# Four edits to the last tenth of an attention and spectral-mix kernel: spectra in tiles of their own, made in spare banks, a first step by halves, each step stored by itself

## The chip, the cores and the metric

One core of a Trainium2 chip. The metric is the device time of one execution in microseconds, the median of several; lower is better. Verdicts use a threshold of 2%. Executions of one kernel spread by 0.6 to 3.4 us, so effects of a few tenths are read from the traces.

## The reference, cut to what matters

Sparse attention over q, k, v (8 batches, 8 heads, 576 positions) gives x of shape (8, 576, 512). Then a spectral layer and a channel mix:

```python
X = np.fft.rfft(x, axis=1)
# 64 modes: Y[:, m] = X[:, m] @ (w_r[m] + i w_i[m])
y = np.fft.irfft(Y, n=S, axis=1)
u = x + y
return (u + np.maximum(u @ w_ch, 0.0)).astype(np.float32)
```

The weights w_r and w_i are 2 x 64 matrices of 512 x 512 in fp32, so most of the time goes into loading them. When the last of them are in, a tail remains: the last spectra, their share in each output row, the relu, the add, and 9.44 MB of stores.

## The kernel before: the parts that matter

The tail works in 20 items. An item is a tile t (128 rows, t = 0 to 3) of two batches, or the last 64 rows (t = 4) of two batches in one tile. Tiles t and t+1 hold the even and the odd rows of one stretch of 256, so partition p of a pair has rows 2p and 2p+1, which lie side by side in DRAM. For each item two PSUM tiles are filled, v (before the relu) and u:

```python
def v_early(k, stop=False):          # own rows, kept in SBUF, through an identity matmul
    vps[k] = psum(("v", "v2")[k % 2], pair=True)
    v_own(k, stop)
def u_early(k): ...                  # the same for u
def new_rows(k, acc, spectra): ...   # share of the last 16 modes, 32-row matmuls

def v_done(k): ...                   # ACT: rl = relu(v), PSUM to SBUF
def u_done(k):                       # DVE: osb = u + rl, then the store
    ...
    if t % 2 == 0:
        osbs[P] = pw.tile([128, 2, 2, DM], FP, tag="w", name="osb")
    osb = osbs[P]
    nc.vector.tensor_tensor(out=osb[:, :, t % 2], in0=up, in1=rls.pop(k), op=AluOp.add)
    for j in range(2):
        dst = out[2 * P + j, ds(128 * (t - t % 2), 256), :].rearrange("(p i) e -> p i e", i=2)
        if k < 4:
            nc.sync.dma_start(dst[:, t % 2], osb[:, j, t % 2])    # rows of 2 KB
        elif t % 2:
            nc.sync.dma_start(dst, osb[:, j])                     # rows of 4 KB, once t and t+1 are in
```

The last spectra, z (times w_ch) and y, for two groups of four batches:

```python
def spec_last(bq, kind):
    both = psum(kind, pair=True)
    spec_mm(3, bq, both[:, 1], both[:, 0])         # z, then y
    act_copy(zzs[bq], both[:, 0])
    nc.vector.tensor_copy(out=yys[bq], in_=both[:, 1])

spec_last(0, "v2")
new_rows(0, vps[0], zzs); new_rows(0, ups[0], yys); v_done(0); u_done(0)
v_early(1); new_rows(1, vps[1], zzs); v_done(1)
spec_last(1, "u")
for k in range(2, LAST + 2):
    v_early(k); u_early(k - 1)
    new_rows(k, vps[k], zzs); new_rows(k - 1, ups[k - 1], yys)
    v_done(k); u_done(k - 1)                       # bounds of k cut here
```

PSUM holds one "v", one "v2" and two "u" tiles of two banks each. Output tiles share five buffers with the weights.

The softmax here doesn't subtract the row's maximum and nothing guards it: scores larger than these inputs give would overflow.

## Time and profile before

| | before |
|---|---|
| time | 435.77 us median (435.15 to 436.52, 3 runs) |
| span of the profiled run | 433.8 us |
| last weights land | 393.92 us |
| last add on DVE ends | 426.75 us |

How to read it: the page divides the span into 40 slices and gives for each the share of time in which the 16 DMA engines were busy (in tenths) and what they moved.

```profile
DMA  8999999999999999999999999999999999991688
GB/s 171 209 212 212 213 213 212 212 211 213 213 212 215 213 213 216 212 215 212 213 212 215 213 213 214 213 214 213 213 213 214 213 214 214 213 187 28 243 323 306
```

The row is full to slice 36: the DMA loads weights without a pause, falls to 28 GB/s in slice 37 while the last spectra are made, and then moves stores, busy for 60 to 80% of each of the last three slices. Only the last four slices can change.

### The profile page before, as it was taken

What the parts mean: (1) busy time and instruction counts of PE and PEld (TensorE: products, weight loads), DVE (VectorE), ACT (ScalarE), POOL (GpSimd) and SP (SyncE); (2) the same over time, 40 slices, a digit from 0 to 9 for tenths busy, and PEclk for the clock granted to TensorE, in tenths of its full rate; (3) what the DMA queues carried; (4) which work ended last, traced back from release to release, by engine and by line L of the source; (5) the groups of instructions that cost most, each with busy time, mean ns of one, the idle gap of its engine ahead of it and who ended that gap; (6) DMA issues with size and microseconds to landing.
All of it is one profiled execution on the core that took longest, in us unless ns stands there. A gap on an engine that the chain in (4) does not pass through costs nothing. (4 is left out here: it accounts for less than half of the span.)

```text
span 433.8 us, 12282 instructions
## 1 busy us (share of the span) xinstructions
PE 347.5 (80%) x5424; PEld 241.5 (56%) x5424; DVE 239.1 (55%) x463; ACT 204.1 (47%) x355; POOL 106.6 (25%) x188
## 2 busy tenths in 40 slices
PE   1987878779988887987487677888799859997992
PEld 1865767558767675776354455655457525554330
DVE  2788768835425444543114355846576455564793
ACT  1587768644545544556141324422343345443671
POOL 5432332322423222222222222222123213210000
PEclk9999989966969998899655899989889959999996
DMA  8999999999999999999999999999999999991688
GB/s 171 209 212 212 213 213 212 212 211 213 213 212 215 213 213 216 212 215 212 213 212 215 213 213 214 213 214 213 213 213 214 213 214 214 213 187 28 243 323 306
DMA packets 29284, 92.18 MB, mean 212 GB/s; under 512 B 4080, under 2 KB 5104, under 8 KB 29232
## 3 DMA queue, kind: packets, MB, share of 16 engines
q0 software_dynamic: 24704, 81.28, 94.5%
q1 hardware_dynamic: 3872, 9.72, 6.0%
q8 instruction: 42, 0.69, 0.6%
q10 hardware_dynamic: 656, 0.41, 0.5%
q14 instruction: 10, 0.08, 0.0%
HBM read 163.22 MB, written 9.44 MB: 398 GB/s over the span
## 5 line engine op out<-in xcount | busy, mean ns | idle before, releaser
L552 PE MATMUL y<-X,wt 128*128 128x16 f16 (+1 forms) x2048 | 82.9, 192 | 30.1 <-DMA wt<-in_moe_w_i_dram 27.5
L552 PEld LDWEIGHTS <-wt 128*128 128x128 f16 (+1 forms) x2048 | 73.3, 101 | 42.4 <-issue 31.8
L201 POOL DMA_DIRECT2D wt<-in_moe_w_r_dram x62 | 36.6, 590 | 173.9 <-PE y L552 93.7
L650 PE MATMUL sc<-w_cp,xT 128*128 128x512 f16 (+1 forms) x160 | 46.7, 419 | 0.0
L201 POOL DMA_DIRECT2D wt<-in_moe_w_i_dram x60 | 35.6, 594 | 43.8 <-DMA wt<-in_moe_w_i_dram 33.4
L659 ACT ACTIVATE v<-sc 128x512 f16<-128x512 f32 x32 | 19.1, 597 | 54.2 <-PE sc L650 54.1
L476 ACT ACTIVATE PL<-sc 128x480 f16<-128x480 f32 (+1 forms) x48 | 27.3, 579 | 33.6 <-PE sc L462 33.4
L660 DVE COPY xo<-tp 128x512 f16<-128x512 f16 x32 | 22.1, 691 | 30.2 <-PE tp L658 30.0
L255 DVE TENSOR_TENSOR xb<-av,rec 90x256 f16<-90x256 f32 (+2 forms) x80 | 36.0, 450 | 2.7
L254 DVE RECIPROCAL rec<-av 90x4 f32<-90x4 f32 (+2 forms) x80 | 14.6, 183 | 33.8 <-PE av L491 22.2
L407 DVE COPY qT<-tp 128x576 f16<-128x576 f16 x16 | 12.0, 758 | 36.6 <-PE tp L400 33.6
L265 ACT ACTIVATE v<-tp 128x640 f16<-128x640 f16 (+1 forms) x24 | 19.4, 808 | 19.7 <-PE tp L434 16.5
L882 DVE TENSOR_TENSOR xo<-u,xo 128x1024 f16<-128x1024 f32 x16 | 19.6, 1225 | 15.2 <-PE u L690 15.1
L400 PE MATMUL tp<-cI_s,ring 64*64 64x64 f16 x864 | 25.0, 204 | 2.0 <-issue 1.2
L365 ACT ACTIVATE PL<-sc 90x360 f16<-90x360 f32 (+1 forms) x48 | 22.8, 490 | 6.6 <-PE sc L358 5.6
L265 ACT ACTIVATE v<-v 128x1024 f16<-128x1024 f32 x16 | 16.4, 1024 | 17.8 <-PE v L690 17.8
L446 PE MATMUL sc<-cMl_s,cI_s 128*128 128x480 f16 (+1 forms) x48 | 21.2, 441 | 3.3 <-ACT X L265 1.6
L400 PEld LDWEIGHTS <-ring 64*64 64x64 f16 x864 | 19.5, 117 | 6.9 <-issue 3.2
L290 PE MATMUL tp<-cI_s,ring 72*128 72x72 f16 x256 | 15.1, 206 | 10.2 <-DMA ring<-in_v_dram 8.6
L519 PEld LDWEIGHTS <-xb 108*128 108x128 f16 (+2 forms) x176 | 15.3, 106 | 12.8 <-DVE xb L255 8.2
L940 ACT ACTIVATE rl<-v 128x1024 f32<-128x1024 f32 (+1 forms) x20 | 18.8, 939 | 7.2 <-PE u L928 5.4
L462 PEld LDWEIGHTS <-kz 128*128 128x128 f16 x160 | 15.3, 111 | 11.6 <-issue 8.1
(114 smaller groups left out, 703.7 us busy)
## 6 DMA issues: line engine op xcount, KB each, us to landing
wt<-in_moe_w_r_dram POOLq DMA_DIRECT2D x62, 512.0 KB, 17.5
wt<-in_moe_w_i_dram POOLq DMA_DIRECT2D x60, 512.0 KB, 19.0
out_dram<-osb SPq DMA_DIRECT2D x12, 512.0 KB, 3.8
ring<-in_v_dram POOLq DMA_DIRECT2D x8, 288.0 KB, 13.3
ring<-in_q_dram POOLq DMA_DIRECT2D x8, 288.0 KB, 13.6
ring<-in_k_dram POOLq DMA_DIRECT2D x8, 288.0 KB, 13.3
out_dram<-osb SPq DMA_DIRECT2D x8, 256.0 KB, 2.6
ring<-in_v_dram POOLq DMA_DIRECT2D x3, 512.0 KB, 14.9
```

Source lines behind the costliest of these rows:

```text
L201: nc.gpsimd.dma_start(dst, rows)
L255: nc.vector.tensor_tensor(out=dst, in0=val.rearrange("p h (q c) -> p h c q", c=4), in1=rec[0:n, 0:pieces] .to_broadcast((n, pieces, 64)) . ...
L265: nc.scalar.activation(out=out, in_=in_, func=ACTF.Copy)
L365: nc.scalar.activation(out=PS[0:n, ds(POFF[t], 4 * n)], in_=scp[0:n, 0 : 4 * n], func=ACTF.Exp, scale=SCALE,)
L400: nc.tensor.transpose(tp[ds(64 * hp, 64), ds(64 * i, 64)], qn[ds(64 * hp, 64), ds(64 * (9 * g + i), 64)], idn[ds(64 * hp, 64), ds(64 * hp, ...
L446: nc.tensor.matmul(scp[:, 0 : n * times].rearrange("p (h x) -> p h x", h=times), idn, mask_rows("cMl", n, times), start=True, stop=False,)
L476: nc.scalar.activation(out=dst, in_=src, func=ACTF.Exp, scale=SCALE)
L552: nc.tensor.matmul(yv[:, mi, e, :], wt[pr, XC[c], ds(128 * e, 128)], Xh[half][pr, c, :, :, m], start=(c == 0), stop=(c == 3),)
L650: nc.tensor.matmul(vp[pr, :], xT[:, ch, cols], w_chs["cp"][:, ch, :], start=(ch == 0), stop=(ch == 3),)
L659: nc.scalar.activation(out=v0[pr], in_=vp[pr, :], func=ACTF.Copy)
L660: nc.vector.tensor_copy(out=xo[pr].rearrange("p (h q c) -> p h q c", h=2, c=4), in_=tp[pr, 0:512].rearrange("p (h c q) -> p h q c", h=2, c=4),
L882: nc.vector.tensor_tensor(out=xo, in0=up[:, 0:n], in1=xo, op=AluOp.add)
```

## The change

Its intent: start the second half of item 0 sooner, give the copies of z and y a tile each so that they don't wait for each other, use banks that stand half empty for the second spectra, and send every item out as soon as it is added. The core of the diff:

```diff
     for bq in range(2):
-        for t in (0, 1, 4, 2, 3) if bq == 0 else (0, 1, 2, 3, 4):
-            items += [(2 * bq, t), (2 * bq + 1, t)]
+        own_t = ((0, 1, 4, 2, 3), (0, 1, 4, 2, 3)) if bq == 0 else ((0, 1, 4, 2, 3), (0, 1, 2, 3, 4))
+        for ts in zip(*own_t):
+            items += [(2 * bq + j, t) for j, t in enumerate(ts)]
 ...  v_done
+        for j in [slice(0, 1), slice(1, 2)] if k == 0 else [slice(0, n)]:
+            nc.scalar.activation(out=rls[k][:, j], in_=vp[:, j], func=ACTF.Relu)
 ...  u_done
+        osb = pw.tile([128, n, DM], FP, tag="w", name="osb")
+        for j in [slice(0, 1), slice(1, 2)] if k == 0 else [slice(0, n)]:
+            nc.vector.tensor_tensor(out=osb[:, j], in0=up[:, j], in1=rl[:, j], op=AluOp.add)
+            if t < 4:
+                rows = out[:, ds(128 * (t - t % 2), 256), :].rearrange("b (p i) e -> p b i e", i=2)
+                bs = slice(2 * P + j.start, 2 * P + j.stop)
+                nc.sync.dma_start(rows[:, bs, t % 2], osb[:, j])
 ...  the tail (spec_z and spec_y are the two halves of spec_mm)
-    spec_last(0, "v2")
+    zp, yp = psum("v2", pair=True)[:, 0], psum("u", pair=True)[:, 0]
+    spec_z(3, 0, zp)
+    spec_y(3, 0, yp)
+    act_copy(zzs[0], zp)
+    nc.vector.tensor_copy(out=yys[0], in_=yp)
     new_rows(0, vps[0], zzs)
+    v_done(0)
+    v_early(1)
     new_rows(0, ups[0], yys)
-    v_done(0)
     u_done(0)
-    v_early(1)
     new_rows(1, vps[1], zzs)
     v_done(1)
-    spec_last(1, "u")
+    u_early(1)
+    new_rows(1, ups[1], yys)
+    u_done(1)
     for k in range(2, LAST + 2):
         if k <= LAST:
             v_early(k)
+        if k == 4:
+            held = vps[k][:, 1]
+            spec_z(3, 1, held)
+        if k == 5:
+            held = vps[k][:, 1]
+            spec_y(3, 1, held)
 ...
+        if k in (4, 5):
+            act_copy((zzs, yys)[k - 4][1], held)
```

## The prediction

> **What bounds the kernel now.** I read the page first, then the chain of waits over the last 54 us, the timeline of each engine there, and the busy time by stretches. The page shows the DMA engines full from the second slice to slice 36 of 40, on the weight loads of the `wt` tiles. The change touches nothing before the last weights, so only what follows can move. Where that begins and what follows is in the chain (start us, us, what):
>
> ```profile
> 382.10 11.81 DMA wt<-in_moe_w_i_dram
> 393.92 0.14 issue
> 394.05 0.64 PE y L552 x16
> ...
> 396.89 0.86 PE v L675 x4
> 397.76 0.24 PE v L671 x4
> 398.00 0.03 ACTq L265
> 398.02 0.04 issue
> 398.07 0.61 ACT zz L265
> 398.67 0.02 issue
> 398.70 0.70 DVE yy L992
> 399.40 0.04 issue
> 399.44 0.39 PE u L928 x2
> ...
> 426.06 0.69 DVE osb L947
> ```
>
> The last weights land at 393.92, the span ends at 433.8: the change lives in 40 us, 9% of the kernel. Two things are to be seen. From 397.76 to 399.44 PE makes the last spectra (L675 z, L671 y), ACT copies z, DVE copies y, strictly one after the other, although the copies read different banks. And the chain stops at the last add, which ends at 426.75, 7 us before the span does. Those 7 us are stores. The stretches show it (us from the start; PE, PEld, DVE, ACT, POOL busy; clock; DMA share; GB/s):
>
> ```profile
> 402.50:403.50 1.00, 1.00 (x9) 0.36 (x8) 0.95 (x2) 0.41 (x2) 0.00 (x0) 1.00 0.99 381
> 406.70:409.80 3.10, 3.10 (x17) 0.92 (x16) 1.88 (x4) 1.90 (x3) 0.00 (x0) 1.00 1.01 382
> 414.50:429.00 14.50, 10.95 (x68) 3.29 (x64) 11.34 (x11) 8.37 (x9) 0.00 (x0) 0.92 1.01 404
> 410.20:412.00 1.80, 1.80 (x14) 0.51 (x12) 1.73 (x2) 1.38 (x2) 0.00 (x0) 1.00 0.89 256
> 412.10:414.20 2.10, 2.10 (x12) 0.63 (x12) 1.94 (x3) 1.81 (x2) 0.00 (x0) 1.00 0.00 0
> 429.60:432.00 2.40, 0.00 (x0) 0.00 (x0) 0.00 (x0) 0.00 (x0) 0.00 (x0) 0.50 0.94 271
> ```
>
> The stores are 9.44 MB. They begin at 402.3, stand wholly still at 412.1 to 414.2 (the kernel there holds a row-pair tile back until both halves are added), and from 414.5 to 429.0 the DMA is full at 404 GB/s, while PE ends at 425.8. So the end is set by when the first store starts, how long the DMA idles between stores, and how fast it moves the bytes. Three speeds are to be seen: 381 to 382 GB/s for rows of 2 KB (the first stores), 404 for rows of 4 KB (the pair stores), 256 to 271 for the 64-row last tiles (t = 4). The costs of the work that feeds them:
>
> ```profile
> L958 DVE TENSOR_TENSOR osb<-u,rl 128x1024 f32<-128x1024 f32 x16 | 19.6, 1224 | 2.6 <-ACT rl L940 0.8 <-PE u L928 0.6
> L940 ACT ACTIVATE rl<-v 128x1024 f32<-128x1024 f32 x16 | 16.4, 1024 | 5.8 <-PE u L928 4.2 <-PE v L928 1.6
> L947 DVE TENSOR_TENSOR osb<-u,rl 128x512 f32<-128x512 f32 x4 | 2.7, 686 | 0.8 <-issue 0.8
> L940 ACT ACTIVATE rl<-v 128x512 f32<-128x512 f32 x4 | 2.4, 598 | 1.4 <-PE u L928 1.2
> ```
>
> **What the Trainium skill says.** "PSUM — Partial Sum Buffer", Specifications: ScalarE and VectorE may read PSUM in parallel at full bandwidth as long as they do not meet in a bank. The trace of before shows them apart only (zz 398.07 to 398.67, yy from 398.70); the program makes DVE wait for ACT because both copies read one tile. Giving z and y separate tiles should let the copies overlap. "VectorE: DVE Perf Modes", the TRN2 errata section, gives an fp32 tensor_tensor add as (N+151)/0.96 ns: 691 and 1224 at N = 512 and 1024; the rows above say 686 and 1224, so it agrees, and halving one add costs about 0.15 us. "ScalarE: Activation LUTs", What ACT_TABLE_LOAD costs, gives an ACTIVATE with immediates as 186 + 0.833 N ns: 612 and 1039 against 598 and 1024 here; halving costs about 0.17 us. "DMA: Bandwidth & Descriptors", Why small descriptors are slow, gives about 3 cycles a packet beside one per 32 bytes; as an estimate that makes 2 KB rows (64+3)/64 over (128+3)/128 = 2% dearer than 4 KB rows. The trace says 404/382 = 6%. The measurement decides.
>
> **The change part by part.** I took the order of the program and its waits for both kernels and walked them with the trace's durations: matmul pairs of L908 and L917 0.43 us, a pair of L928 0.32, an add 0.11 us after its rows of u end, a store's first bytes 0.8 us after its issue (401.45 to about 402.3).
>
> (1) Tiles of their own. ACT can start on z at 397.83 instead of 398.07 (the y matmuls take 0.24), DVE copies y at 398.07 to 398.76 instead of 398.70 to 399.39. The own rows of item 1 (L908, 0.43) fill PE's wait for yy. Rows of v begin at 398.47 instead of 398.71, rows of u at 399.22 instead of 399.44.
>
> (2) First step by halves. ACT relu 398.90 to 399.50 and to 400.10. DVE adds 399.68 to 400.37 and to 401.06; before, one add ran 400.20 to 401.43. The first 256 KB go out at 400.4 instead of 401.45, the second at 401.1. First bytes: 401.2 instead of 402.3, worth 1.1 us.
>
> (3) Second step at once, last spectra later. Before, PE made the second spectra (1.26 us) and DVE their yy copy (0.69) ahead of item 1's add, which ended at 404.4. After: own rows of u 399.86, relu 400.12 to 401.14, add 401.19 to 402.42: 2.0 us earlier. The second spectra (0.87 + 0.24) move into the half-used banks of items 4 and 5, which have one bank each. The work on PE is the same, so this gain is paid back: walking on, the adds end at 404.22, 406.39, 407.18, 408.48, 410.54 for items 2 to 6, where before they ended at 405.7, 407.0, 407.7, 409.0, 410.9. From item 6 on PE runs at 1.30 us an item in both, 0.3 us ahead of before. DVE loses one 0.69 copy to ACT, which has room (8.37 busy of 14.5). The last add ends at about 426.3 instead of 426.75.
>
> (4) Each step stored by itself. Item 6 is stored at 410.56 instead of 413.49, so the 2.1 us of standstill go. Against that all whole items now have 2 KB rows: 512 KB at 385 GB/s are 1.36 us, at 407 they were 1.29.
>
> The DMA's ledger. Before: first byte 402.3, idle 1.3 + 0.45 + 2.1 = 3.9 to 4.0, busy 8 x 0.68 + 12 x 1.29 + about 4.2 for the last tiles = 25.1, with small gaps 25.7; last byte 432.0. After: first byte 401.2; idle 0.65 (402.6 to 403.25), 0.45 (404.6 to 405.05), 0.8 (406.4 to 407.2), 0.9 (410.5 to 411.4) = 2.8; busy 16 x 1.36 + 4.2 = 26.0; last byte 430.0. The gain is 1.1 (start) + 1.2 (idle) - 0.9 + 0.6 (rows of 2 KB, less the small gaps that the before ledger carries and the after ledger does not) = 2.0 us. From item 6 on the ledger has the DMA without a pause for 18 to 19 us: it makes 1.36 an item where PE and DVE need 1.30, so 0.3 us more or less on the engines changes nothing at the end. What follows the last byte (432.0 to 433.8) stays. 435.77 - 2.0 gives 433.7.
>
> **The rivals.** First: the end follows the engines, and their 0.4 us is all there is (435.3). For it: DVE is busy 11.34 of the 12.25 us in which it still worked in that stretch, and PE all but without a pause. Against it: 7 us of stores after the last add. Second: the 2 KB rows eat the gain. All 8.4 MB at 382 would be 22.0 us against 20.9 now; if the three-level stores also issue slowly (the 64-row ones took SP 0.54 us and more, the 128-row ones 0.33), or with the DMA below 380, the end comes at 435 to 436. Nothing of before has this form of store, so I can't exclude it. Third: output tiles. Before used 12 of them, after uses 20 from the same five buffers, so an add must wait for the store five items back. By my ledger store k-5 lands 0.8 to 1.5 us before add k needs its buffer, so no wait; if it comes, the DMA has four stores queued at that time and the end hardly moves, by 0.5 us at most. Fourth, upward: the DMA does better than 385 once stores stand end to end, or idles less early; then 405 GB/s leaves 1.0 us more (432.7).
>
> **Range and chances.** The executions of before spread by 1.4 us, as much as most of what is in question. I take 433.7, with 432.5 (fourth rival and a quicker start) to 435.2 (first or second). A gain of 2% is 8.7 us, more than the 7 us of stores after the last add and over four times my sum: 1 in 100. A loss of 2% would need the stores at about two thirds of their speed: 1 in 100.
>
> **What would show it.** Right: zz and yy copies overlap near 398; the first store at about 400.4; item 1 added by 402.4; no DMA standstill after 411.5; last byte near 430.0 at about 385 GB/s from 411.5 on; the last add near 426.3. Wrong: a wait of the adds for stores; a rate under 375 in that stretch; standing DMA between 404 and 411 of more than 3 us; PE held at the own rows of u in items 2 to 5 by more than 0.3 us; or weights that land at another time than 393.9, which the change gives no reason for.

## The result, and the profile after

433.81 us median (432.90 to 434.26, 4 runs) against 436.14 us for before on the same chip (435.15 to 436.73, 4 runs): 0.9946, interval 0.9920 to 0.9973. By its interval it is a gain of about 0.5%. Ratios are the mean time of one kernel's fast runs over that of the other's of the same rounds, so not quite the ratio of the medians.

The chain of waits of the changed kernel, where the tail begins (start us, us, what):

```profile
393.69 0.64 PE y L552 x16
...
396.45 1.52 PE v L912 x4
397.97 0.88 PE v L669 x4
...
398.92 0.61 ACT zz L265
```

Beside the same lines of before (L675 and L908 there; shown in the prediction), z (L669) starts 1.1 us later although the weights were 0.4 us earlier. The four own-row matmuls of L912 took 1.52 us where before had 0.86: TensorE was at half clock just here. The busy times of the changed kernel show it (us from the start; PE, PEld, DVE, ACT, POOL busy with counts; granted clock; DMA share; GB/s):

```profile
390.80:394.20 3.40, 1.76 (x22) 0.93 (x22) 1.85 (x3) 0.65 (x2) 0.00 (x0) 1.00 0.33 65
394.20:397.70 3.50, 3.50 (x29) 1.59 (x26) 0.29 (x1) 0.00 (x0) 0.00 (x0) 0.51 0.00 0
```

and before in the same places:

```profile
390.80:394.20 3.40, 2.29 (x29) 1.21 (x28) 2.38 (x3) 1.62 (x2) 0.00 (x0) 1.00 0.37 75
394.20:397.70 3.50, 3.50 (x46) 2.07 (x44) 0.29 (x1) 0.00 (x0) 0.00 (x0) 1.00 0.01 1
```

No edit touches that stretch, and a second trace of the changed kernel (below) has the full clock there and is 0.8 us shorter. Half clock comes and goes between traces: those of u_tiles and no_u_own (below) have 3.4 us of it at this place, those of u_spectra and u_halves 6.8 us of it that end at 393.3 and 394.3, and the others none from 385 on until the last matmuls are done. So tails are compared from a mark that this can't reach: the start of the z copy (ACT zz). The copies of the changed kernel overlap now, DVE's start lying 0.18 us after ACT's, and each takes as long as it did alone (0.60 and 0.69 us); ACT's relus and DVE's adds of the end follow:

```profile
398.92 0.60 ACT L265 ACTIVATE zz<-v 128x512 f16<-128x512 f32 x1 [6.57 <-PE v L669]
```
```profile
399.10 0.69 DVE L991 CAST yy<-u 128x512 f16<-128x512 f32 x1 [2.32 <-PE u L676]
400.92 2.42 DVE L954 TENSOR_TENSOR osb<-u,rl 128x512 f32<-128x512 f32 x3 [1.13 <-PE v L932]
...
410.04 10.38 DVE L954 TENSOR_TENSOR osb<-u,rl 128x1024 f32<-128x1024 f32 x8 [0.64 <-PE u L932]
...
421.93 5.79 DVE L954 TENSOR_TENSOR osb<-u,rl 128x1024 f32<-128x1024 f32 x5 [0.64 <-PE u L932]
```

The stores of the changed kernel in the same columns as before:

```profile
411.70:412.20 0.50, 0.50 (x7) 0.10 (x4) 0.50 (x1) 0.50 (x1) 0.00 (x0) 1.00 0.22 57
412.20:423.00 10.80, 10.80 (x66) 3.29 (x64) 9.47 (x9) 7.82 (x9) 0.00 (x0) 1.00 1.00 378
429.50:431.00 1.50, 0.00 (x0) 0.00 (x0) 0.00 (x0) 0.00 (x0) 0.00 (x0) 0.50 0.81 240
```

The 2.1 us of standstill have become a quarter of a microsecond at 412. From then on the DMA is full, at 378 GB/s where before had 404, and the last byte lands at 430.9, 3.2 us after the last add (427.72). DVE's waits hold no store at all (us in total, times, longest):

```profile
...
DVE osb L954 <- PE u L932: 3.2, 5, 1.0
DVE yy L991 <- PE u L676: 2.3, 1, 2.3
DVE osb L954 <- PE v L932: 1.1, 1, 1.1
DVE osb L954 <- ACT rl L946: 0.6, 1, 0.6
```

### The profile page after: what moved, and what is told of

It is laid out like the page before. It is cut to its first block, busy times and chain, and to the rows that moved or that the text cites.

```text
span 432.3 us, 12285 instructions
## 1 busy us (share of the span) xinstructions
PE 350.1 (81%) x5424; PEld 243.6 (56%) x5424; DVE 238.9 (55%) x463; ACT 204.6 (47%) x357; POOL 106.2 (25%) x188
## 5 line engine op out<-in xcount | busy, mean ns | idle before, releaser
L552 PE MATMUL y<-X,wt 128*128 128x16 f16 (+1 forms) x2048 | 82.3, 192 | 31.3 <-DMA wt<-in_moe_w_i_dram 29.4
L552 PEld LDWEIGHTS <-wt 128*128 128x128 f16 (+1 forms) x2048 | 72.6, 101 | 44.1 <-issue 34.2
L476 ACT ACTIVATE PL<-sc 128x480 f16<-128x480 f32 (+1 forms) x48 | 27.4, 578 | 32.8 <-PE sc L462 32.3
L954 DVE TENSOR_TENSOR osb<-u,rl 128x1024 f32<-128x1024 f32 (+1 forms) x21 | 22.1, 1070 | 5.8 <-PE u L932 3.2
L519 PEld LDWEIGHTS <-xb 108*128 108x128 f16 (+2 forms) x176 | 16.5, 112 | 12.6 <-DVE xb L255 7.9
```

The costliest lines, as they stand in the source:

```text
L476: nc.scalar.activation(out=dst, in_=src, func=ACTF.Exp, scale=SCALE)
L552: nc.tensor.matmul(yv[:, mi, e, :], wt[pr, XC[c], ds(128 * e, 128)], Xh[half][pr, c, :, :, m], start=(c == 0), stop=(c == 3),)
L954: nc.vector.tensor_tensor(out=osb[:, j], in0=up[:, j], in1=rl[:, j], op=AluOp.add)
```

## The experiments

The question was which part brought the gain. Two theories went into the runs, and each expectation says what each of them forecasts. The ledger theory is the prediction's own way of adding up: an earlier first store, less idle, slower rows, each worth what it moves. The tight-point theory: from item 6's store on the DMA never pauses, so the end is that store's start plus the bytes left, and what happens earlier counts only if it moves that store.

Two numbers are taken from each trace: when item 6's add starts, and when the span ends, both from the start of the z copy. Where z and y share a tile (before, "u_tiles", "only_each", "min_best") ACT starts after the y matmuls, and their 0.24 us are added to both. Spans are taken to a hundredth from the traces. These two numbers repeat: the two traces of the changed kernel differ by 0.02 us in them.

| run | median us | ratio to before of its rounds | item 6's add | end of span |
|---|---|---|---|---|
| before | 435.4 to 436.3 | 1 | 11.80 | 35.97 |
| changed kernel | 433.81 | 0.9946 (0.9920 to 0.9973) | 11.12 | 33.34 |
| changed kernel again | 433.53 | 0.9943 (0.9919 to 0.9967) | 11.12 | 33.36 |
| u_pairs | 435.63 | 0.9989 (0.9969 to 1.0008) | 11.12 | 35.87 |
| u_spectra | 432.84 | 0.9930 (0.9915 to 0.9945) | 10.83 | 33.02 |
| u_halves | 433.76 | 0.9952 (0.9934 to 0.9971) | 11.12 | 33.39 |
| u_tiles | 434.11 | 0.9962 (0.9946 to 0.9977) | 11.75 | 33.96 |
| only_each | 433.34 | 0.9940 (0.9915 to 0.9966) | 11.79 | 34.05 |
| rows4k (wrong result) | 432.73 | 0.9921 (0.9894 to 0.9949) | 11.12 | 32.88 |
| no_u_own (wrong result) | 433.04 | 0.9928 (0.9903 to 0.9952) | 9.24 | 32.79 |
| own_first | 433.44 | 0.9943 (0.9912 to 0.9975) | 11.12 | 33.31 |
| best1 | 432.36 | 0.9925 (0.9897 to 0.9953) | 10.83 | 32.98 |
| best2 | 432.36 | 0.9921 (0.9893 to 0.9949) | 10.83 | 33.24 |
| min_best | 434.24 | 0.9965 (0.9933 to 0.9997) | 11.78 | 34.19 |

The runs of one call share a chip and the runs of before: u_pairs to u_tiles, the second look to no_u_own, and own_first to min_best. These were timed against before in 5 rounds each, the changed kernel's first row with 4 executions of each kernel.

**u_pairs: pair stores back.** In u_done of the changed kernel, for t < 4 and from item 4 on:

```diff
+        if t < 4 and k >= 4:
+            if t % 2 == 0:
+                osbs[P] = pw.tile([128, 2, 2, DM], FP, tag="w", name="osb")
+            osb = osbs[P]
+            nc.vector.tensor_tensor(out=osb[:, :, t % 2], in0=up, in1=rl, op=AluOp.add)
+            if t % 2:    # both batches, rows of 4 KB
+                ...
+            return
```

> The changed kernel with pair stores again from item 4 on (rows of 4 KB, a tile held back until both its steps are added). Two theories from here on. Ledger theory (as in the prediction): the parts of the gain add up, 1.1 us for the earlier first store, 1.2 for less idle, 0.9 lost to 2 KB rows; this run then loses 2.1 and wins 0.9 back: the end 1.2 us later than the changed kernel. Tight-point theory: from item 6's store on the DMA never pauses, so the end is (first bytes of item 6's store) plus the bytes left, and what happens earlier counts only if it moves that store. Here the DMA then stands until the add of item 8 ends, about 2.6 us later, and moves 12 whole items at 1.29 us and two half ones: 1.5 to 1.7 us later than the changed kernel, about 435.4, with a standstill of about 2 us near 412.

The gain is all but gone: 0.9989, and the tail 2.5 us longer in the trace. The standstill is back and longer than before's:

```profile
411.40:414.10 2.70, 2.70 (x21) 0.86 (x20) 2.54 (x3) 2.15 (x3) 0.00 (x0) 1.00 0.00 0
```

Both theories had less (1.2, and 1.5 to 1.7); the ledger is the farther off. Part of what the tight-point theory missed is a second pause near the end, while a pair waits for its second half: between 425.5 and 426 the DMA's share is 0.04. Item 6 is added at the same time as in the changed kernel, so neither PE nor DVE has to do with it.

**u_spectra: second spectra where before had them.**

```diff
     v_done(1)
-    u_early(1)
-    new_rows(1, ups[1], yys)
-    u_done(1)
+    both = psum("u", pair=True)
+    spec_z(3, 1, both[:, 0]); spec_y(3, 1, both[:, 1])
+    act_copy(zzs[1], both[:, 0])
+    nc.vector.tensor_copy(out=yys[1], in_=both[:, 1])
     ... (the loop as before)
```

> The changed kernel with the second spectra made right after item 1's rows of v, in a tile of u, with DVE's copy of y (as before). The add of item 1 goes back by 1.3 to 2 us. If the second step at once is worth what it moves, the end comes 1 us or more later. Tight-point theory: the PE work ahead of item 6 is the same, item 6's store moves by 0.3 us at most, and so does the end: 433.8 to 434.2.

Both theories missed the sign: it is faster than the changed kernel, by 0.3 us in the trace, and item 6 is 0.29 us earlier (the intervals of the two ratios overlap, so the times alone don't show it). PE's order shows why. First the changed kernel (its second trace), then this run; each line is start, duration, engine, line, what, count:

```profile
399.94 0.60 PE L921 MATMUL u<-xo,cI_s 128*128 128x512 f16 x2
400.48 0.39 PE L932 MATMUL u<-yy,cFl_s 32*128 32x512 f16 x2
400.80 0.61 PE L912 MATMUL v<-v,cI_s 128*128 128x512 f16 x2
401.34 0.39 PE L932 MATMUL v<-zz,cFl_s 32*128 32x512 f16 x2
```
```profile
401.81 0.59 PE L921 MATMUL u<-xo,cI_s 128*128 128x512 f16 x2
402.34 0.39 PE L932 MATMUL v<-zz,cFl_s 32*128 32x512 f16 x2
402.34 0.39 PE L932 MATMUL u<-yy,cFl_s 32*128 32x512 f16 x2
402.66 0.60 PE L912 MATMUL v<-v,cI_s 128*128 128x512 f16 x2
```

The rows of v of item k and of u of item k-1 read four different groups of 32 rows. Side by side (402.34) the four matmuls take PE 0.32 us together; apart (400.48 and 401.34) they take 0.32 us twice. Where one of the two items is a 64-row one and the other is not, they take 0.32 us each even one right after the other (404.57 and 404.90 in the changed kernel's second trace), in both kernels. Finishing item 1 at once takes one such pair apart. It is bought with 0.3 us on PE, and what it buys, item 1's add 1.2 us earlier (it ends 4.42 us after the z copy, here 5.59), is worth nothing at the end.

**u_halves: first step whole.** Both `[slice(0, 1), slice(1, 2)] if k == 0 else [slice(0, n)]` become `[slice(0, n)]`.

> The changed kernel with the first step whole: one relu, one add, one store of 512 KB, first bytes about 0.8 us later. Ledger theory: the end 0.8 us later. Tight-point theory: item 6's store does not move, the DMA only idles less between items 0 and 6, the end stays within 0.2 us.

The end moves by 0.03 to 0.05 us in the trace; the ratio, 0.9952, is inside the interval of the changed kernel. The first bytes came 0.75 us later from the z copy, and the DMA made up for it by idling less up to item 6: its share is 0.86 in that stretch here and 0.77 in the changed kernel's (first this run, then the second trace of the changed kernel).

```profile
403.60:412.40 8.80, 8.80 (x54) 2.93 (x52) 5.83 (x7) 6.41 (x9) 0.00 (x0) 1.00 0.86 299
```
```profile
401.70:411.40 9.70, 9.70 (x62) 3.30 (x60) 6.66 (x7) 7.24 (x9) 0.00 (x0) 1.00 0.77 273
411.40:429.90 18.50, 14.29 (x84) 4.30 (x80) 13.89 (x13) 10.47 (x12) 0.00 (x0) 0.94 1.00 367
```

This is the run that tells the theories apart most cleanly: the ledger had 0.8, the tight point 0.

**u_tiles: one tile for z and y.**

```diff
-    zp, yp = psum("v2", pair=True)[:, 0], psum("u", pair=True)[:, 0]
+    both = psum("v2", pair=True)
+    zp, yp = both[:, 0], both[:, 1]
```

> The changed kernel with z and y in one tile again: ACT waits for the y matmuls (0.24 us), DVE for ACT, and PE's own rows of item 1 for both copies, so the rows of u of item 0 start about 0.6 us later and every item after it. Both theories: item 6 and the end about 0.6 us later, zz and yy copies one after the other in the trace.

As expected, 0.6 us in the trace, for item 6 and for the end alike. The copies are one after the other again: ACT's starts at 399.73 and takes 0.60 us, DVE's starts at 400.36, released by it. (This trace, too, has half clock just before, so its absolute times are late.)

**after_again: the changed kernel.**

> The changed kernel itself once more, for the rounds of the other three: ratio to before 0.9946 as first measured (0.992 to 0.9973), and a second trace of it: from the start of the z matmuls to the last store byte 32.8 us again, whatever the clock does before.

The ratio repeats (0.9943). I had counted 32.8 us from the z matmuls to the last byte of SP's queue; it was 32.7, and 0.25 more with the last half tile, which goes out on ACT's queue and which that count had left out.

**only_each: the kernel before with one edit, each step stored by itself.**

```diff
-        if t % 2 == 0:
-            osbs[P] = pw.tile([128, 2, 2, DM], FP, tag="w", name="osb")
-        ...
+        osb = pw.tile([128, 2, DM], FP, tag="w", name="osb")
+        nc.vector.tensor_tensor(out=osb, in0=up, in1=rls.pop(k), op=AluOp.add)
+        rows = out[:, ds(128 * (t - t % 2), 256), :].rearrange("b (p i) e -> p b i e", i=2)
+        nc.sync.dma_start(rows[:, 2 * P : 2 * P + 2, t % 2], osb)
```

> The kernel before with one part alone: each step stored by itself. Ledger theory: 2.1 us of standstill saved, 0.9 paid for rows of 2 KB: 1.2 us faster than before. Tight-point theory: item 6 is stored at the end of its own add (2.6 us earlier than now), then 18.3 us of stores without a pause: 1.7 to 2.0 us faster than before, nearly the whole gain of the change; from the z matmuls to the last byte 33.2 us.

0.9940: by the times, this edit alone is as good as the whole change; in the trace it has 1.9 of its 2.6 us. Item 6's add stands where before has it (11.79 and 11.80), so all of it comes from the store.

**rows4k: the same bytes in rows of 4 KB.** The result is wrong: every item is written into one closed stretch, so rows land in the wrong places and some rows stay unwritten.

```diff
-                nc.sync.dma_start(rows[:, bs, t % 2], osb[:, j])
+                flat = out[2 * P + t % 2, ds(128 * (t - t % 2), 256), :].rearrange("(p i) e -> p (i e)", i=2)
+                nc.sync.dma_start(flat, osb.rearrange("p i e -> p (i e)"))     # k > 0
```

> Wrong result on purpose: the changed kernel with each step stored into one stretch of 4 KB rows, same bytes, same times of issue. If the DMA bounds the part after item 6, 0.07 us an item over 12 items come off until the engines bind: 0.7 to 1.2 us faster than the changed kernel, the rate above 395 GB/s where it is not waiting. If the engines set the end: no change.

0.5 us in the trace, and 0.95 us by the ratios of these rounds (0.9921 against 0.9943); the rate is 398 GB/s:

```profile
411.40:422.00 10.60, 10.60 (x67) 3.29 (x66) 9.27 (x9) 7.76 (x9) 0.00 (x0) 1.00 0.99 398
```

So the short rows do cost, and the DMA does bind from item 6 on: with the adds at the same times from the z copy as in the changed kernel, the end comes earlier. The intervals of the two ratios overlap; the 0.5 us rests on the trace. The run makes the rows longer and the stretch that they fill closed, both at once, and doesn't tell the two apart.

**no_u_own: 0.43 us less of PE an item.** The own rows are left out of u.

```diff
     def u_early(k):
         ups[k] = psum("u", pair=True)
-        for j, r in enumerate(own(items[k], xos, xoh)):
-            nc.tensor.matmul(ups[k][:, j], idn, r, start=True, stop=False)
```

> Wrong result on purpose: the own rows of u are not added on PE (0.43 us an item less). PE is then at about 0.87 to 1.1 us an item, DVE at 1.26. Tight-point theory: item 6's store comes about 1.7 us earlier and the DMA binds from there: the end 1.3 to 2.0 us earlier than the changed kernel. If PE set the end all along, 20 items at 0.43 less down to DVE's 1.26 would move the last add by 2.2 us and the end with it. The idle of the DMA ahead of item 6 falls below 1.5 us.

A miss for both theories. Item 6 is added 1.9 us earlier, but the end moves by 0.6 only, and the adds now wait for stores (us in total, times, longest):

```profile
DVE osb L952 <- DMA out_dram<-osb: 1.0, 3, 0.7
```

The tight point has moved. With item 6 that early the DMA is still busy with items 3 to 5, two of them the slow 64-row tiles, so item 6's store stands in a queue. The tight-point theory holds for item 6 only between 11.8 and about 10.8 us after the z copy; that is the range in which all the other kernels lie.

**own_first, best1, best2, min_best: can both kernels be beaten?** PE waits for the last weights for over a microsecond, and the own rows of item 0 stood behind that wait. The move:

```diff
     for i, (slot, m) in enumerate(rest):
+        if i == NL:
+            v_early(0, True); v_own(0, True); v_own(0); u_early(0)
         mode(slot, m)
         ...
-        if i == NL:
-            v_early(0, True); u_early(0)
-        elif i > NL:
-            v_own(0, True)
-    v_own(0)
```

> The changed kernel with the matmuls of item 0's own rows (the same number of them) moved ahead of the last weights, into PE's wait for them. In the trace of before they stand between the last two groups of L552 and after them: the last weights land at 395.07 but their L552 starts at 395.55, and z starts at 396.89 though YT is ready at 396.36. If the end is a fixed stretch after the z matmuls (32.7 us to the last byte), it comes as much earlier as z does: 0.8 to 0.9 us, ratio to before near 0.9925. If the DMA's own backlog or the weights set it, less than 0.3. The clock may spoil it[...].

> The same move, with the second spectra back where they were before (as in the run that undid that part, whose item 6 was 0.3 us earlier because the rows of v of item 2 and of u of item 1 then run side by side on PE). Both gains added: z 0.8 to 0.9 earlier, 32.4 us from z to the last byte: about 1.2 us faster than the changed kernel, ratio near 0.991. If only one tight point can bind, no more than the better of the two alone.

> As the run before it, and the second 64-row store of every last tile goes out from ACT's queue beside the first on SP's, instead of after it. In the traces these tiles move at 0.48 to 0.53 MB in 2 us with the DMA busy all that time (whole items: 0.76). If that is because only half of the partitions are read at a time, two stores side by side run at 380 GB/s and the tile at item 14 costs 0.3 us less: 0.3 faster than the run before it. If the rate is the 64-row form's own, no change.

> The kernel before with two edits alone: each step stored by itself, and the own rows of item 0 ahead of the last weights. 33.7 us from z to the last byte as in the run with the first edit alone, and z 0.8 to 0.9 us earlier: ratio near 0.992.

own_first is a miss: its ratio is that of the changed kernel. Its trace shows the z copy 1.47 us after the start of the last YT add (L580, which completes the input of the last spectra), where the second trace of the changed kernel has 1.78, so of the 0.8 to 0.9 us about 0.3 came; the own rows now hold PE until 394.56, and the last groups of L552 (the matmuls with the weights) start only then. best1 (this move with u_spectra) has the fastest median with best2, 432.36 us, and a tail as short as u_spectra's plus that 0.3. Its interval overlaps the changed kernel's, so a gain over it is shown by the traces and not by the times. best2 (best1 with the second 64-row store on ACT's queue) is not faster: by the times of its packets the 64-row tile of item 14 moves at 269 GB/s with its two stores side by side, and at 265 one after the other in best1. Its tail is 0.26 us longer, but not by its edit: up to the last item the two traces agree within 0.05 us, and the last item, which goes out on both queues in either run, took 1.24 us here and 0.98 in best1 (1.12 and 1.14 in the two traces of the changed kernel). So a difference of 0.2 us between two ends can be the last item's alone. Why 64-row stores are slower than whole items at 378 stays open.

min_best (only_each with the move) came out at 0.9965 with an interval that nearly reaches 1, less than only_each in other rounds (0.9940); its tail from the z copy is only_each's within 0.14 us. By the times nothing can be said of the move in it.

## Why the prediction was right, and where its steps failed

The total was right: 433.7 forecast, 433.81 measured; in part that is luck, as the terms below show. The mechanism held: stores end the kernel, and a tile that is held back leaves the DMA standing. Item 6's first bytes move 16.50 us after the z copy in before and 13.27 us after it in the changed kernel (counted as in the table), and from there on neither DMA stands still; less what the shorter rows cost, that is the gain. Most of the walk was right too. Set against the second trace of the changed kernel, whose clock was full, and counted from the z matmuls, the copies of z and y and the first rows of v came within 0.1 us of the forecast, the adds of items 1 to 5 within 0.25, the last byte 0.1 earlier (32.98 against 33.1). One sign of being wrong that the prediction named did come: the last weights landed at 393.55 in one trace of the changed kernel and at 395.52 in the other, not at 393.9. As two traces of one kernel differ by 2 us there, it says nothing of the change.

Step (1), tiles of their own: right. Undone, it costs 0.6 us, and the copies overlap at their old durations.

Step (2), the first step by halves, "worth 1.1 us": wrong as a term of the sum. The first store did go out earlier, but undoing the halves moves the end by 0.05 us at most. The bytes that go out sooner leave the DMA idle before item 6 instead.

Step (3), second step at once and spare banks: the sum said that the gain is paid back and PE is 0.3 us ahead at item 6. It was 0.7 ahead (11.12 against 11.80). Undone, tiles of their own are worth 0.63 of it and this part costs 0.29; that leaves 0.34, which no run undoes alone. PE's order fits it: before had item 1's own rows between the rows of u of item 0 and the rows of v of item 1, the change puts them ahead of both, and that pair now stands together (before, then the second trace of the changed kernel):

```profile
399.44 0.39 PE u L928 x2
399.83 0.54 PE v L908 x2
400.37 0.32 PE v L928 x2
```
```profile
399.68 0.32 PE u L932 x2
400.00 0.01 PE v L932 x2
```

The forecast held that "the work on PE is the same" and missed that the rows of v of one item and of u of another share 0.32 us when they stand together: the change makes one such pair (item 0) and breaks one (item 1).

Step (4), each step stored by itself: the sign was right, the size was not. The forecast had 2.1 less 0.9 for short rows, 1.2 in all. Alone it gave 1.9 us, undone it cost 2.5. The short rows cost 0.5 us in the trace and 0.95 by the times, whose intervals overlap.

So the total came out of terms whose errors cancel: 1.1 too much at the start, about as much too little at the stores. A further 0.6 us of the forecast's 2.0 is bookkeeping: its ledger of before carries small gaps, that of after none. And one sentence of it fell: that "0.3 us more or less on the engines changes nothing at the end". Between the runs with item 6 at 11.79, 11.75, 11.12 and 10.83 us the end goes with item 6 one for one: 34.05, 33.96, 33.35, 33.02. A full DMA hides the engines' work behind its starting point, not ahead of it.

The first rival (the engines set the end) fell: from the z copy the last add ends after 28.80 us, where before had 28.92 with the same 0.24 added, and the end came 2.6 us earlier. The second, that short rows eat the gain, was real in kind but too small. The third, waits for output tiles, did not come in the changed kernel and came (1.0 us in all) once PE was made lighter. The fourth, above 385 GB/s, fell: the rate was 378.

## What to carry to other kernels

When stores set the end of a kernel, find the last moment at which their queue ran dry: the end is that moment plus the bytes that follow, and only work that moves that moment is worth anything, until another moment becomes the last one (here once item 6 came 1.9 us earlier). Holding a finished tile back to make rows longer pays only where the queue has other stores to send meanwhile; here 4 KB rows bought 5% of rate and cost 2 us of standing still. And don't add up "earlier starts": test each by undoing it alone, since a total can be right with its terms wrong.

## What the Trainium skill lacked or had wrong

- "DMA: Bandwidth & Descriptors", Why small descriptors are slow: from its cycles I estimated rows of 2 KB at 2% dearer than rows of 4 KB. These stores ran at 378 GB/s with 2 KB rows and at 398 to 404 with 4 KB rows, 5 to 7%.
- "TensorE: Matmul & The Clock Gate", Why this matters for your kernels, asks for no idle gaps over about 3 us. Here one wait of 1.54 us was followed by 3.4 us at half clock, when PE had been busy for 1.76 of the 3.4 us before (clock 0.51, the four L912 matmuls 1.52 us in place of 0.86). In the trace of before, with 2.29 of 3.4 in about the same place, the clock stayed full. No threshold follows from the pair: earlier in that trace (317.6 to 321.0) PE was busy for 2.35 of 3.4 us, and the next 3.4 us ran at half clock.
